# Engine queues written out task by task, and the weights' loads behind the second batch's x, in a spectral-filter and gated-unit kernel

## The chip, the cores and the metric

The kernel runs on one core of a Trainium2 chip. The metric is device time in microseconds (us) of one execution. Five engines matter: PE (TensorE, matmuls), DVE (VectorE), ACT (ScalarE), POOL (GpSimd, which here issues the loads of inputs) and SP (SyncE, which issues the scratch transfers and the stores). Each works through its own list of instructions in order and waits on semaphores for the others.

## What is computed

Eight batches of x, 3200 x 256, are filtered along the sequence by a real Fourier transform, a pointwise complex filter and the inverse transform. The result goes through a gated unit: a causal convolution of five taps per channel gives a gate, a sigmoid is taken of it, and it multiplies a projection; a second projection gives the output.

```python
X = np.fft.rfft(x, axis=1)
y = np.fft.irfft(X * (filt_r + 1j * filt_i)[None, :, :], n=x.shape[1], axis=1)
yp = np.concatenate([np.zeros((B, K - 1, D)), y], axis=1)
gate_pre = sum(conv_w[k] * yp[:, k:k + S, :] for k in range(K))
return (1 / (1 + np.exp(-gate_pre)) * (y @ w_val)) @ w_out
```

## The kernel before, in words

The transform of length 3200 is split as 100 x 32. For each batch b, in the names of the plan's tasks (the number after the comma counts the pieces):

- `lx` (L286, POOL): eight loads of x into `xt` tiles, of which there are ten, with a cast to bf16.
- `s1` (L548, PE): eight products of an x tile with the table cf_t. `so` (L539 on ACT, L541 on DVE): their evacuation from PSUM into one tile `so`.
- `t` (L567, DVE): four transposes of `so` into `tt`.
- `s2` (L577, PE), `xs` (L539 or L541), `z` (L593, DVE, multiplication with the filter tile f_t), `ia` (L608, PE, first half of the inverse) and `ue` (L539 or L541, evacuation into `u`): seven pieces each, the last one of half the size.
- The way from `u` to `vt`: batch 0 is turned by four transposes on DVE (`k`, L649). Batches 1 to 7 write `u` to a scratch in memory (`wr`, L631, SP) and read it back in another order (`lv`, L641 and L642, SP).
- `ib` (L659, PE) and `ye` (L668, ACT): the second half of the inverse, eight pieces, into `yt`. `ha` (L675, POOL) clears the four columns ahead of it.
- Then seven blocks of the sequence: `cv` (the convolution, L698, or L712 for pairs of blocks in batches 6 and 7), `ga` (sigmoid, L722, ACT), `vl` (L732, PE, reads the weights wv_t), `gv` (L747, DVE), `op` (L755, PE, reads the weights wo_t), `oe` (evacuation, L539 or L541) and `st` (store, L770, SP).

At the start there are tables to make (cf_t, w_t, a_t, b_t, ci_t, dg_t), the filters to load (L346, L349, L352, POOL, in two halves), and eight copies `fd` of filter halves to further partitions (ACT or DVE; they write f_t). `te` are the evacuations of a_t and b_t (`tp` are their matmuls), `dg` makes the ten small tables dg_t (L523, ACT), and `cim` makes ci_t (two products on DVE). `pd` (L624, POOL) clears a part of `u` for batch 0.

PSUM is used as four slots of 128 x 1024 in float32. Each PE task takes one (a pair of blocks takes two), and the evacuation gives it back. The tasks `so`, `xs`, `ue`, `oe`, `te` and `fd` may run on ACT or on DVE.

The order of instructions on every engine is made by a planner in the kernel's own program (class `Plan`), run once when the kernel is built. Each task has a cost per engine it may use, the tasks it depends on, buffers that it takes and gives, and a landing time for transfers. Before the change each task also has a rank, from a list of numbers TIMES. At each step the planner looks at all tasks that are ready and takes the one with the lowest rank, with a penalty STAY for a change of the PE array's mode and LEAN for DVE where ACT could do the task. The instructions are then written in that order with `manual_schedule`, which leaves it as it is. Transfers are planned on one line called DQ. These planned times are not measured ones; only the order reaches the chip.

The eleven weight loads are one task on POOL, `wts`, which the plan may begin, like the first x load of batch 1, when the task `pool` (a fixed number in the code) says that POOL is free. The order that results on POOL is: the filters' loads, `lx1,0`, `wts`, `lx1,1`, `pd0`, `lx1,2` and so on.

The first tasks that the queues hold before, where the change reaches them:

- DVE, after the tables: te3,0 fd0,0,0 t0,0 te1,0 fd0,1,1 t0,1 fd0,1,0 t0,2 fd1,0,0 cim t0,3 fd1,1,1 xs0,0 fd1,1,0 z0,0 z0,2 z0,1 ue0,2 z0,3 z0,4 z0,5 so1,2 xs0,6 z0,6 so1,4 k0,0 k0,1 k0,2 k0,3 t1,0
- PE, from the first s2: s20,0 s20,1 s11,0 s20,2 ia0,0 s20,3 ia0,2 s20,4 s11,1 ia0,1 s20,5 s11,2 ia0,3 s20,6 ia0,4 ia0,5 s11,3 s11,4 ia0,6 s11,5 s11,6 s11,7 ib0,0

(`s11,2` is piece 2 of s1 of batch 1, `s20,5` piece 5 of s2 of batch 0; `fd1,0,1` is the second half's first filter, second copy.)

Of the kernel before, what the change touches and what calls it, by code (L numbers as in the profile page):

```python
# [24 lines left out]
STAY, LEAN = 2.6, 5.1  # L25

TIMES = [6045, -2430, 3242, -301, 64, -3062, 3825, -4640, -1646, -3299, -5370, 2181, -2530, 351,
# [90 lines left out]
NCH = R // RC  # L118
# [828 lines left out]
```

## Time and profile before

| | |
|---|---|
| median of three runs | 304.4 us (303.82 to 306.0) |
| the profiled execution | 303.57 us, its span 301.8 us |
| busy: PE, DVE, ACT, POOL | 258.3, 263.6, 256.2, 63.0 us |
| granted TensorE clock, mean | 0.985 |
| transfers | 66.00 MB, mean 219 GB/s |

The span runs from the first to the last instruction; the time of the execution holds 1.8 us more around it. Busy time is what an engine spends in instructions. A matmul's end is modelled, so a busy PE need not be at its peak. In rows of the order of time the columns are start, length (both us), engine, line, operation, tiles written and read, count, and in brackets the idle time before it and what ended it. Rows of groups give the total busy time and the mean of one in ns.

### The profile page before, as it was taken

To read this page: it belongs to the slowest core of one execution; us is meant where nothing else is said; L and a number is where in the kernel's file an instruction comes from. 1 tells how busy PE (TensorE), PEld (TensorE's weight loads), DVE (VectorE), ACT (ScalarE), POOL (GpSimd) and SP (SyncE) were. 2 spreads that over 40 slices of the span, in tenths; PEclk is the share of its full clock that TensorE was granted. 3 is DMA by queue.
4 is the path that set the end of the run, shared out by engine and by line. 5 is a ranking of instruction groups with operands and counts; after the bars stand their busy time and mean duration, and the time that the engine had idled before them with its cause. 6 is when DMAs were issued, how large, how long until landed. Compare 5 with 4: busy or idle time off the path is not lost.

```text
span 301.8 us, 9355 instructions
## 1 busy us (share of the span) xinstructions
PE 258.3 (86%) x3924; PEld 156.8 (52%) x3924; DVE 263.6 (87%) x294; ACT 256.2 (85%) x299; POOL 63.0 (21%) x122
## 2 busy tenths in 40 slices
PE   2822492778999899989999999999999999999991
PEld 0111340634555654666466465747666677766661
DVE  7979959898999999999999999999999984766761
ACT  3997775699789997999999999999999889787652
POOL 8699953022023002300320300000000000000000
PEclk9999998799999999999999999999999999999998
DMA  6998699469689997999999997998563799875375
GB/s 91 190 112 103 79 166 186 79 94 182 173 244 269 252 305 179 222 282 359 198 237 316 289 212 205 331 311 288 174 231 121 233 292 341 280 292 208 125 292 204
DMA packets 52874, 66.00 MB, mean 219 GB/s; under 512 B 7712, under 2 KB 34208, under 8 KB 52832
## 3 DMA queue, kind: packets, MB, share of 16 engines
q1 hardware_dynamic: 40624, 50.09, 49.2%
q0 software_dynamic: 12208, 15.31, 32.7%
q8 instruction: 31, 0.51, 0.7%
q14 instruction: 11, 0.09, 0.1%
HBM read 42.54 MB, written 38.14 MB: 267 GB/s over the span
## 4 chain that ended last, share of the span: by engine, by line
PE 48%; DMA 14%; DVE 14%; POOL 9%; ACT 8%; issue 6%; SPq 0%; DVEq 0%; POOLq 0%; ACTq 0%
PE ps L755 11%; PE ps L698 11%; PE ps L732 11%; DMA vt<-escr 8%; PE ps L659 5%; PE ps L608 4%; DVE gv L747 3%; DVE so L541 3%; PE ps L712 3%; DMA out_dram<-o 3%; DMA f_t<-in_filt_r_dram 2%; PE ps L548 2%; POOL xt L286 2%; ACT so L539 2%; DVE vt L649 2%
## 5 line engine op out<-in xcount | busy, mean ns | idle before, releaser
L747 DVE TENSOR_TENSOR gv<-ps,gt 128x1024 bf16<-128x1024 f32 (+1 forms) x56 | 60.8, 1103 | 13.5 <-PE ps L732 10.1
L593 DVE TENSOR_TENSOR z<-xs,f_t 128x2048 bf16<-128x2048 bf16 (+1 forms) x56 | 62.7, 1138 | 4.3 <-ACT xs L539 4.1
L722 ACT ACTIVATE gt<-ps 128x1024 bf16<-128x1024 f32 (+1 forms) x56 | 52.1, 945 | 10.4 <-PE ps L712 5.8
L286 POOL DMA_DIRECT2D xt<-in_x_dram x64 | 36.4, 570 | 108.6 <-PE ps L548 89.3
L668 ACT ACTIVATE yt<-ps 128x800 bf16<-128x800 f32 x64 | 52.1, 846 | 7.0 <-PE ps L659 6.5
L548 PE MATMUL ps<-xt,cf_t 100*128 100x512 bf16 x128 | 43.5, 424 | 11.6 <-DMA xt<-in_x_dram 9.3
L755 PE MATMUL ps<-wo_t,gv 128*128 128x256 bf16 x400 | 51.8, 273 | 0.8 <-DVE gv L747 0.4
L732 PE MATMUL ps<-yt,wv_t 128*128 128x512 bf16 (+1 forms) x224 | 51.9, 356 | 0.0
L698 PE MATMUL ps<-yt,dg_t 64*64 64x512 bf16 (+1 forms) x880 | 48.7, 348 | 0.4
L539 ACT ACTIVATE so<-ps 128x1024 bf16<-128x1024 f32 x42 | 42.2, 1042 | 6.6 <-PE ps L548 4.2
L539 ACT ACTIVATE u<-ps 128x1024 bf16<-128x1024 f32 (+1 forms) x41 | 40.0, 982 | 4.7 <-PE ps L608 4.3
L755 PEld LDWEIGHTS <-gv 128*128 128x128 bf16 x400 | 36.8, 97 | 12.2 <-issue 3.0
L539 ACT ACTIVATE o<-ps 128x1024 f32<-128x1024 f32 (+1 forms) x37 | 36.8, 999 | 6.2 <-PE ps L755 5.3
L659 PE MATMUL ps<-ci_t,vt 104*128 104x100 f16 (+1 forms) x512 | 33.7, 213 | 8.8 <-DVE vt L649 6.5
L567 DVE STREAM_TRANSPOSE tt<-so 128x1024 f32<-128x1024 f32 x32 | 38.7, 1227 | 0.6 <-ACT so L539 0.6
L539 ACT ACTIVATE xs<-ps 128x1024 bf16<-128x1024 f32 (+1 forms) x36 | 35.3, 998 | 3.6 <-PE ps L577 3.3
L659 PEld LDWEIGHTS <-vt 104*128 104x128 bf16 (+1 forms) x512 | 28.4, 101 | 19.0 <-DVE vt L649 7.1
L698 PEld LDWEIGHTS <-dg_t 64*64 64x64 bf16 x880 | 24.3, 106 | 15.4 <-issue 4.3
L608 PE MATMUL ps<-z,a_t 64*64 64x256 bf16 x416 | 28.4, 289 | 4.5 <-ACT gt L722 1.9
L577 PE MATMUL ps<-tt,w_t 64*64 64x256 bf16 x416 | 23.5, 293 | 9.4 <-DVE tt L567 8.5
L608 PE MATMUL ps<-z,b_t 64*64 64x256 bf16 x416 | 28.1, 283 | 0.0
L732 PEld LDWEIGHTS <-wv_t 128*128 128x128 bf16 x224 | 19.0, 97 | 17.3 <-issue 3.2
(98 smaller groups left out, 225.1 us busy)
## 6 DMA issues: line engine op xcount, KB each, us to landing
out_dram<-o SPq DMA_DIRECT2D x48, 512.0 KB
xt<-in_x_dram POOLq DMA_DIRECT2D x64, 200.0 KB, 7.3
escr<-u SPq DMA_DIRECT2D x42, 256.0 KB
vt<-escr SPq DMA_DIRECT2D x56, 192.0 KB
out_dram<-o SPq DMA_DIRECT2D x8, 128.0 KB
escr<-u SPq DMA_DIRECT2D x7, 128.0 KB
vt<-escr SPq DMA_DIRECT2D x56, 16.0 KB
f_t<-in_filt_r_dram POOLq DMA_DIRECT2D x2, 112.0 KB, 3.6
```

The lines of the kernel that those rows point to most:

```text
L286: nc.gpsimd.dma_start(out=xt[0:L], in_=src)
L539: nc.scalar.activation(dst, src, AF.Copy, **kw)
L548: nc.tensor.matmul(ps[:, 512 * h:512 * h + 512], lhsT=cf_t[0:L].rearrange("p h c i -> p (h c i)"), rhs=xv[:, DQ // 2 * h:DQ // 2 * h + DQ ...
L593: nc.vector.tensor_tensor(z[:, :, :, 0:nm * D], st.pop(("XS", b, u))[:, :, 0:nm * D].unsqueeze(1) .to_broadcast((128, 2, 2, nm * D)), f_t[ ...
L608: nc.tensor.matmul(ps[64 * h:64 * h + 64, 512 * t + D * a:512 * t + D * a + D], lhsT=tab[rows, h, m0 + a, :], rhs=z[rows, w, h, D * a:D * ...
L659: nc.tensor.matmul(ps[:, o:o + L], lhsT=v[rows, RC * j + a, 128 * dh:128 * dh + 128], rhs=ci_t[rows, way, :], start=True, stop=True)
L668: nc.scalar.activation(y[:, :, H:H + N].rearrange("p h (a r) -> p h a r", r=R)[:, :, :, RC * j:RC * j + RC], ps[:, :].rearrange("p (h n) - ...
L698: nc.tensor.matmul(ps[o:o + 64, 512 * dh:512 * dh + w], lhsT=dg_t[rows, dh, k, :], rhs=y[rows, dh, BLK * c + k:BLK * c + k + w], start=(k ...
L722: nc.scalar.activation(g[:, :, 0:w], two_banks(ps, w), AF.Sigmoid)
L732: nc.tensor.matmul(ps[:, 512 * eh:512 * eh + w], lhsT=wv_t[:, dh, eh, o:o + 128], rhs=y[:, dh, H + BLK * c:H + BLK * c + w], start=(dh == ...
L747: nc.vector.tensor_tensor(o, i0, i1, op=ALU.mult)
L755: nc.tensor.matmul(ps[:, D * a:D * a + D], lhsT=gv_[:, eh, 128 * a:128 * a + 128], rhs=wo_t[:, c % 2 * pair(b, c), eh, :], start=(eh == 0) ...
```

## The change

The list of ranks and the choice among ready tasks go. In their place stand five lists, QUEUES, one each for PE, DVE, ACT, POOL and SP, that name the tasks (by their number in the order in which they are added) in the order in which the engine works them. So they also hold which of ACT and DVE does a task. The planner now only begins the first task of each line when it can, to find in which order to write out the instructions of the engines and which PSUM slot a task gets. Tasks without an engine and transfers are chosen as before.

The weights' task is split in two, `wv` (four loads) and `wo` (seven loads). In POOL's new queue `wv` stands behind `lx2,4` and `wo` behind `lx2,7`; before them come `lx1,0 pd0 lx1,1` to `lx1,7` and `lx2,0` to `lx2,4`. The first `vl` and the first `op` now depend on them in the plan. The first `s1` of a batch depends on the last one of the batch before. The landing times of the filters' parts, of the time at which POOL comes free and of the transfers' line are other numbers.

The new queues of the head, in the same names:

- DVE, after the tables: t0,0 t0,1 t0,2 t0,3 fd0,1,1 fd0,0,0 fd0,1,0 z0,0 fd1,0,0 z0,1 z0,2 fd1,1,0 fd1,0,1 fd1,1,1 z0,4 z0,3 z0,5 z0,6 ue0,5 k0,0 k0,1 k0,2 cim k0,3 t1,0
- PE, from the first s2: s20,0 tp2 s20,1 ia0,0 s20,2 s20,3 ia0,1 s11,0 ia0,2 s20,4 s20,5 s11,1 ia0,4 s20,6 ia0,3 ia0,5 ia0,6 s11,2 s11,3 s11,4 s11,5 s11,6 s11,7 ib0,0
- ACT, from the last so of batch 0: fd0,0,1 te1,0 te0,0 te1,1 te0,1 xs0,0 cia te2,0 xs0,1 te2,1 te3,0 xs0,2 xs0,3 ue0,0 ue0,1 so1,0 xs0,4 xs0,5 te3,1 ue0,2 xs0,6 ue0,4 ue0,3 ue0,6 dg0 so1,3 so1,2 so1,1 so1,4 so1,6 so1,5 so1,7 ye0,0

Over the whole kernel the tasks that stand in ACT's queue go from 289 to 299, in DVE's from 237 to 227; `so` goes from 42 to 52 on ACT and from 22 to 12 on DVE, and the copy `fd1,0,1` goes from ACT to DVE. PE's 406 tasks are the same, in another order.

```diff
 SMALL = (6, 7)
-STAY, LEAN = 2.6, 5.1
-TIMES = [6045, -2430, 3242, -301, 64, -3062, 3825, -4640, -1646, -3299, -5370, 2181, -2530, 351,
...
+QUEUES = dict(
+    PE=[0, 2, 4, 6, 8, 10, 12, 1557, 14, 1554, 1563, 21, 1560, 26, 24, 31, 36, 29, 142, 34, 41,
+           46, 146, 44, 51, 39, 49, 54, 150, 154, 158, 162, 166, 170, 60, 62, 64, 66, 68, 70, 177,
...
+    DVE=[1549, 1551, 1553, 1566, 16, 17, 18, 19, 1543, 1540, 1542, 23, 1544, 28, 33, 1546, 1545,
...
+    ACT=[1550, 3, 5, 7, 1, 9, 1552, 13, 1570, 11, 15, 1541, 1558, 1555, 1559, 1556, 22, 1567,
...
+    POOL=[140, 20, 144, 148, 152, 156, 160, 164, 168, 338, 342, 346, 350, 354, 1521, 358, 362, 76,
...
+    SP=[182, 190, 198, 206, 214, 230, 222, 83, 234, 252, 237, 240, 243, 249, 92, 246, 255, 404,
...
-    def __init__(self, room, slots, times, stay=1.0, lean=0.0):
-        self.tasks, self.room, self.stay = {}, dict(room), stay
-        self.lean, self.slots, self.times = lean, list(range(slots)), iter(times)
+    def __init__(self, room, slots, queues):
+        self.tasks, self.room, self.queues = {}, dict(room), queues
+        self.slots = list(range(slots))
 
     def add(self, name, engines, deps, emit, take=(), give=(), land=0.0, mode=None,
             ps=0, free=()):
-        queue = engines.keys() - {"none", "DQ"}
-        rank = next(self.times) / 100 if queue else 0.0
-        self.tasks[name] = dict(engines=engines, rank=rank, deps=deps, emit=emit, take=take,
+        self.tasks[name] = dict(engines=engines, deps=deps, emit=emit, take=take,
                                 give=give, land=land, mode=mode, ps=ps, free=free, slots=[],
                                 at=len(self.tasks))
 
     def run(self):
+        names = list(self.tasks)
+        lines = {e: [names[i] for i in q] for e, q in self.queues.items()}
...
+        def can(n):
+            t = self.tasks[n]
+            return (need[n] == 0 and ready_at[n] <= now + 1e-9 and len(self.slots) >= t["ps"]
+                    and all(self.room[p] >= t["take"].count(p) for p in t["take"]))
+
+        def begin(n, e):
...
-            best = None
-            for n in ready:
...
-                for e, cost in t["engines"].items():
-                    if free.get(e, 0.0) <= now + 1e-9:
-                        away = e == "PE" and t["mode"] != mode
-                        other = e == "DVE" and len(t["engines"]) > 1
-                        key = (round(t["rank"] + (self.stay if away else 0.0)
-                                     + (self.lean if other else 0.0), 6), cost, t["at"])
...
+            went = left
+            for n in [n for n in loose["none"] if can(n)]:
+                if can(n):
+                    loose["none"].remove(n)
+                    begin(n, "none")
+            if left < went:
...
+            for e, line in lines.items():
+                if line and free.get(e, 0.0) <= now + 1e-9 and can(line[0]):
+                    begin(line.pop(0), e)
...
-    def load_w():
+    def load_wv():
         for dh in range(2):
             src = moe_w_val[128 * dh:128 * dh + 128, :].rearrange("p (e j) -> p e j", e=2)
             nc.gpsimd.dma_start(out=wv_t[:, dh, :, 0:128], in_=src)
             nc.gpsimd.dma_start(out=wv_t[:, dh, :, 128:224], in_=src[:, :, 0:96])
+
+    def load_wo():
         for s in range(2):
...
-    plan = Plan(dict(xt=NXT, so=1, t=1, xs=3, z=3, u=1, e=2, v=1, y=2, g=NGB, gv=NGB, o=NOB), 4, TIMES,
-                stay=STAY, lean=LEAN)
+    plan = Plan(dict(xt=NXT, so=1, t=1, xs=3, z=3, u=1, e=2, v=1, y=2, g=NGB, gv=NGB, o=NOB), 4, QUEUES)
...
-                add(f"lx{b},{j}", {"POOL": 0.6}, ["pool"] + ([f"lx{b},{j - 1}"] if j else [f"lx{b - 1},{NCH - 1}"] if b > 1 else []),
+                add(f"lx{b},{j}", {"POOL": 0.6}, ["pool"] + (
+                    [f"lx{b},{j - 1}"] if j else [f"lx{b - 1},{NCH - 1}"] if b > 1 else []),
                     lambda e, b=b, j=j: load_x(b, j), take=("xt",), land=1.5)
                 add(f"dx{b},{j}", {"DQ": 1.22}, [f"lx{b},{j}"], None, land=2.0, mode=1)
             dep = [f"dx{b},{j}"] if b else [f"x0{j}", "cfa"]
-            dep = dep + ([f"s1{b},{j - 1}"] if j else [])
+            dep = dep + ([f"s1{b},{j - 1}"] if j else [f"s1{b - 1},{NCH - 1}"] if b else [])
             add(f"s1{b},{j}", {"PE": 0.45}, dep, lambda e, b=b, j=j: s1(b, j),
...
-                [f"cv{b},{p}"] + ([f"vl{b},{c - 1}"] if c else []), lambda e, b=b, c=c: val(b, c),
+                [f"cv{b},{p}"] + ([f"vl{b},{c - 1}"] if c else [] if b else ["wvq+"]), lambda e, b=b, c=c: val(b, c),
...
-            add(f"op{b},{c}", {"PE": 0.88 * f}, [f"gv{b},{c}"],
+            add(f"op{b},{c}", {"PE": 0.88 * f}, [f"gv{b},{c}"] + ([] if b or c else ["woq+"]),
...
-    add("pool", {"none": 0.0}, [], None, land=22.0)
-    add("wts", {"POOL": 5.0}, ["pool"], lambda e: load_w())
+    add("pool", {"none": 0.0}, [], None, land=24.4)
+    add("wv", {"POOL": 4.2}, ["pool"], lambda e: load_wv())
+    dma("wvq", 2.4, ["wv"], land=2.0, mode=1)
+    add("wo", {"POOL": 3.4}, ["wv"], lambda e: load_wo())
+    dma("woq", 2.6, ["wo"], land=2.0, mode=1)
     for j in range(NCH):
         add(f"x0{j}", {"none": 0.0}, [], None, land=4.5 + 1.3 * j)
-    add("dq", {"DQ": 23.5}, [], None, mode=0)
-    for n, when in (("fr0,0", 16.5), ("fr0,1", 19.6), ("fr1,0", 22.8), ("fr1,1", 25.8)):
+    add("dq", {"DQ": 25.5}, [], None, mode=0)
+    for n, when in (("fr0,0", 16.3), ("fr0,1", 20.0), ("fr1,0", 23.3), ("fr1,1", 27.0)):
         add(n, {"none": 0.0}, [], None, land=when)
```

More of the change, by code (lines that the diff above doesn't have):

```diff
@@ L144, in run @@
     def run(self):
-        left = dict(self.tasks)
+        names = list(self.tasks)
+        lines = {e: [names[i] for i in q] for e, q in self.queues.items()}
         users, need = {}, {}
-        for n, t in left.items():
+        for n, t in self.tasks.items():
             need[n] = len(t["deps"])
@@ L150, in run @@
                 users.setdefault(d, []).append(n)
-        ready_at = {n: 0.0 for n in left}
-        free = {}
+        ready_at = {n: 0.0 for n in names}
+        loose = {e: [n for n in names if e in self.tasks[n]["engines"] and need[n] == 0]
+                 for e in ("none", "DQ")}
+        free, gives, order = {}, [], []
         mode = turn = None
-        gives = []
-        ready = {n for n in left if need[n] == 0}
-        order = []
-        now = 0.0
+        now, left = 0.0, len(names)
+        def can(n):
[3 more added lines that the diff above has]
+        def begin(n, e):
+            nonlocal mode, turn, left
+            t = self.tasks[n]
+            cost = t["engines"][e]
+            for p in t["take"]:
+                self.room[p] -= 1
+            t["slots"] = [self.slots.pop(0) for _ in range(t["ps"])]
+            if e == "PE":
+                cost += 0.1 if t["mode"] != mode else 0.0
+                mode = t["mode"]
+            if e == "DQ":
+                turn = t["mode"]
+            end = now + cost
+            done = end + SEM.get(e, 0.1)
+            if e != "none":
+                free[e] = end
+            back = list(t["give"]) + [self.tasks[o]["slots"][i] for o, i in t["free"]]
+            if back:
+                gives.append((done, back))
+            for u in users.get(n, ()):
+                need[u] -= 1
+                ready_at[u] = max(ready_at[u], done + t["land"])
+                for k in loose:
+                    if need[u] == 0 and k in self.tasks[u]["engines"]:
+                        loose[k].append(u)
+            left -= 1
+            order.append((t["emit"], e, t["slots"], now, end))
         while left:
@@ L190, in run @@
-            if best is None:
-                later = [ready_at[n] for n in ready if ready_at[n] > now + 1e-9]
-                later += [v for v in free.values() if v > now + 1e-9]
-                later += [g[0] for g in gives if g[0] > now + 1e-9]
-                assert later, ("stuck", sorted(ready)[:20], self.room)
-                now = min(later)
-                continue
-            _, n, e, cost = best
-            t = left.pop(n)
-            ready.discard(n)
-            for p in t["take"]:
-                self.room[p] -= 1
@@ L202, in run @@
-            t["slots"] = [self.slots.pop(0) for _ in range(t["ps"])]
-            if e == "PE":
-                if t["mode"] != mode:
-                    cost += 0.1
-                mode = t["mode"]
-            if e == "DQ":
-                turn = t["mode"]
-            end = now + cost
-            free[e] = end
-            done = end + SEM.get(e, 0.1)
-            back = list(t["give"]) + [self.tasks[o]["slots"][i] for o, i in t["free"]]
-            if back:
-                gives.append((done, back))
@@ new lines, in run @@
+            for e, line in lines.items():
+                if line and free.get(e, 0.0) <= now + 1e-9 and can(line[0]):
+                    begin(line.pop(0), e)
+            if free.get("DQ", 0.0) <= now + 1e-9:
+                here = [n for n in loose["DQ"] if can(n)]
+                if here:
+                    n = min(here, key=lambda n: (
+                        round(ready_at[n] + (1e4 if self.tasks[n]["mode"] == turn else 0.0), 6),
+                        self.tasks[n]["at"]))
+                    loose["DQ"].remove(n)
+                    begin(n, "DQ")
@@ L221, in run @@
+            if left < went:
+                continue
+            later = [v for v in free.values() if v > now + 1e-9] + [g[0] for g in gives]
+            later += [ready_at[n] for n in loose["none"] + loose["DQ"]]
+            later += [ready_at[line[0]] for line in lines.values() if line and need[line[0]] == 0]
+            later = [v for v in later if v > now + 1e-9]
+            assert later, ("stuck", {e: line[:1] for e, line in lines.items()}, self.room)
+            now = min(later)
         self.span = max(free.values())
@@ L912 @@
         sp_setup()
-        for emit, e, slots in order:
+        for emit, e, slots, _, _ in order:
             st["slots"] = list(slots)
```

22 lines of the change are left out of this document (removed), and 158 rows, old and new, of tables (ACT, DVE, PE, POOL).

## The prediction

> **What bounds the kernel now.** I read the page first, for the load of each engine, then the busy time by stretches, for where each is full.
>
> ```profile
> span 301.8 us, 9355 instructions
> PE 258.3 (86%) x3924; PEld 156.8 (52%) x3924; DVE 263.6 (87%) x294; ACT 256.2 (85%) x299; POOL 63.0 (21%) x122
> ```
>
> ```profile
> 27.30:46.90 19.60, 14.32 (x171) 7.49 (x172) 15.28 (x15) 13.74 (x16) 15.66 (x26) 1.00 0.88 127
> 46.90:60.00 13.10, 6.08 (x77) 4.78 (x76) 11.96 (x9) 7.51 (x10) 1.37 (x4) 0.74 0.70 128
> 60.00:210.00 150.00, 142.32 (x2092) 83.89 (x2087) 146.16 (x135) 140.97 (x164) 21.48 (x42) 1.00 0.92 246
> 210.00:250.00 40.00, 40.00 (x684) 26.78 (x674) 38.34 (x38) 37.42 (x44) 0.21 (x2) 1.00 0.65 218
> 250.00:290.00 40.00, 39.97 (x814) 27.54 (x813) 25.58 (x25) 30.04 (x35) 0.10 (x1) 1.00 0.69 252
> 290.00:301.80 11.80, 5.26 (x40) 3.33 (x38) 3.11 (x4) 4.90 (x5) 0.00 (x0) 0.90 0.58 226
> ```
>
> Three engines carry nearly the same load. The columns of the second view are window, length, then busy time of PE, weight loads, DVE, ACT and POOL. From 60 to 210 DVE is the fullest (146.2 of 150), from 210 to 290 PE is never idle, and the end (from 290) is a drain. The empty time is at the head: from 27.3 to 60 PE works 20.4 of 32.7 us. A head that ends earlier brings the full part forward by as much, unless the full part itself grows.
>
> Who sets the pace in the head is told by the order of time on POOL, PE, DVE and ACT:
>
> ```profile
> 24.49 1.33 POOL L286 DMA_DIRECT2D xt<-in_x_dram  x1
> 25.81 0.76 POOL L359 DMA_DIRECT2D wv_t<-in_moe_w_val_dram  x1
> 27.26 1.33 POOL L359 DMA_DIRECT2D wv_t<-in_moe_w_val_dram  x1
> 29.27 1.65 POOL L365 DMA_DIRECT2D wo_t<-in_moe_w_out_dram  x2
> 33.63 0.56 POOL L286 DMA_DIRECT2D xt<-in_x_dram  x1 [0.16 <-issue]
> 34.17 1.40 POOL L624 MEMSET u<- 128x1536 bf16 x1
> 35.50 4.38 POOL L286 DMA_DIRECT2D xt<-in_x_dram  x8
> ```
>
> ```profile
> 27.38 1.07 PE L577 MATMUL ps<-tt,w_t 64*64 64x256 bf16 x16 [8.52 <-DVE tt L567]
> 37.35 1.03 PE L548 MATMUL ps<-xt,cf_t 100*128 100x512 bf16 x2 [2.45 <-DMA xt<-in_x_dram]
> 54.18 3.92 PE L659 MATMUL ps<-ci_t,vt 128*128 128x100 f16 x55 [3.25 <-DVE vt L649]
> ```
>
> ```profile
> 18.20 1.25 DVE L567 STREAM_TRANSPOSE tt<-so 128x1024 f32<-128x1024 f32 x1 [0.58 <-ACT so L539]
> 24.62 1.08 DVE L541 COPY f_t<-f_t 32x3584 bf16<-32x3584 bf16 x1
> 25.72 0.46 DVE L303 TENSOR_SCALAR ci_t<-sx,wt 128x100 f16<-128x100 f32 x2
> 26.08 1.24 DVE L567 STREAM_TRANSPOSE tt<-so 128x1024 f32<-128x1024 f32 x1
> 27.35 1.09 DVE L541 COPY f_t<-f_t 32x3584 bf16<-32x3584 bf16 x1
> 41.41 1.23 DVE L593 TENSOR_TENSOR z<-xs,f_t 128x2048 bf16<-128x2048 bf16 x1 [3.16 <-ACT xs L539]
> 46.90 3.71 DVE L649 STREAM_TRANSPOSE vt<-u 128x1024 f32<-128x1024 f32 x2 [0.44 <-ACT u L539]
> ```
>
> ```profile
> 22.31 1.29 ACT L523 ACTIVATE dg_t<-j,cw 128x64 bf16<-128x64 f16 x5
> 39.43 1.02 ACT L539 ACTIVATE u<-ps 128x1024 bf16<-128x1024 f32 x1 [3.10 <-PE ps L608]
> 46.66 2.89 ACT L539 ACTIVATE so<-ps 128x1024 bf16<-128x1024 f32 x3
> 54.98 2.29 ACT L668 ACTIVATE yt<-ps 128x800 bf16<-128x800 f32 x3 [5.43 <-PE ps L659]
> ```
>
> Two things stretch the head. First, PE idles 8.52 us because the four turns of batch 0 (L567) run from 18.20 to 27.32 on DVE: filter copies and other work stand between them in DVE's queue. Second, eleven weight loads hold POOL from 25.81 to 33.5, so the second x tile of batch 1 is issued at 33.63 and PE, which works its queue in order, waits 2.45 us for it at 37.35. That wait is handed on: ACT idles 3.10 and DVE 3.16 behind it. The next fixed point is 46.90, where batch 0's second turn (L649) begins.
>
> **The change, part by part.** Durations come from the groups, shapes kept apart:
>
> ```profile
> L567 DVE STREAM_TRANSPOSE tt<-so 128x1024 f32<-128x1024 f32 x32 | 38.7, 1227 | 0.6 <-ACT so L539 0.6
> L593 DVE TENSOR_TENSOR z<-xs,f_t 128x2048 bf16<-128x2048 bf16 x48 | 57.4, 1216 | 4.2 <-ACT xs L539 4.1
> L541 DVE COPY f_t<-f_t 32x3584 bf16<-32x3584 bf16 x3 | 3.3, 1084 | 0.1
> L541 DVE COPY f_t<-f_t 32x3072 bf16<-32x3072 bf16 x3 | 3.0, 991 | 0.1
> L539 ACT ACTIVATE f_t<-f_t 32x3584 bf16<-32x3584 bf16 x1 | 3.2, 3187 | 0.0
> L593 DVE TENSOR_TENSOR z<-xs,f_t 128x1024 bf16<-128x1024 bf16 x8 | 5.3, 668 | 0.1
> L539 ACT ACTIVATE so<-ps 128x1024 bf16<-128x1024 f32 x42 | 42.2, 1042 | 6.6 <-PE ps L548 4.2
> L541 DVE CAST so<-ps 128x1024 bf16<-128x1024 f32 x22 | 26.2, 1216 | 1.3 <-ACT yt L668 1.1
> ```
>
> *Head, DVE's queue.* The new queue puts the four turns first and the filter copies behind them. The turns wait for the last so evacuation as before, so they start at 18.2 and end at 18.2 + 4 x 1.23 = 23.1 in place of 27.3. Between the first turn and L649 the new queue holds 4 turns (4.91), 3 first-half copies (2.97), all 4 second-half copies (4.34; one came from ACT, where it took 3.19), 6 full z (7.30), the short z (0.67) and one u evacuation (1.2): 21.4 us. The old queue held 24.7 there and took 46.90 - 18.20 = 28.7, so 4.0 of it was idle (3.16 in one piece, behind the x wait). With no idle L649 would begin at 39.6, 7.3 earlier; with the same 4.0, at 43.6, 3.3 earlier. The x wait should go, but DVE still depends on ACT and on four PSUM slots, so I take the middle: 5.3 earlier. The two ci_t products (0.46) move into the middle of the L649 turns, which gives back 0.5: **-4.8**.
>
> *Head, behind that point.* ACT must now do dg_t (1.29) and seven so of batch 1 (0.96 each by the run of three) between L649's start and the first yt: 8.0 us. Before, the first yt began 54.98 - 46.90 = 8.1 after it. Nothing is gained or lost here: 0, between -0.5 and +0.5.
>
> *x tiles of batch 1.* Seven issues and the 1.40 memset follow the filters at once, from 25.8: the second tile about 27.2 in place of 33.63. It was used 3.7 us after issue (33.63 to 37.35), so it can be used from 31. In the new PE queue that tile's matmuls stand behind the second half of the s2 and ia work, which z paces to past 33. The 2.45 wait goes, inside the -4.8.
>
> *Weights.* The value weights now stand behind the thirteenth x issue after batch 0 (the fifth tile of batch 2), which needs the buffer of batch 1's third tile; PE reads that right before L649's start, at about 41. The four issues took 25.81 to 29.27, 3.5 us; the output weights' seven took 29.27 to 33.5, 4.2 us, and follow the last x of batch 2. Landing took 4.1 and 4.3 us:
>
> ```profile
> wv_t<-in_moe_w_val_dram POOLq DMA_DIRECT2D x2, 48.0 KB, 4.1
> wo_t<-in_moe_w_out_dram POOLq DMA_DIRECT2D x1, 64.0 KB, 4.3
> 73.08 1.04 PE L732 MATMUL ps<-yt,wv_t 128*128 128x512 bf16 x4
> ```
>
> Value weights are there by 41 + 0.6 + 3.5 + 4.1 = 49, output weights by about 57. The first reader was at 73.08 and comes to 68: 19 us of cover. Behind them on POOL the last three x of batch 2 come 3.5 later and batch 3's first 4.2 later; both are read 8 us and more after that. Cost 0; were the cover gone, the eleven issues would cost up to 7.7.
>
> *The steady part.* Nothing is added for PE: 406 tasks in both, and the mode of the array changes 143 times for 147. ACT and DVE exchange work. Ten so move from DVE to ACT; u and xs move about as much between them. By the groups' means, over the whole kernel DVE loses 9.7 us and ACT gains 6.5. Of this DVE loses 5.1 between its last L649 turn and batch 4's last gv (54 to 240), and ACT gains 4.3 between the first yt of batch 0 and of batch 6 (55 to 244). If DVE alone bound the stretch it would shrink by 5.1; if ACT did, it would grow by 4.3. From 60 to 210 DVE has 146.2 now and would have about 141, ACT 141.0 and would have 145.3: the fullest engine falls by 0.9. I take **-0.9**.
>
> Here a rule decides whether PE matters. PE is 95% busy from 60 to 210 with 2092 matmuls in 150 us, 13.9 per us, and 100% busy from 210 to 250 with 17.1 per us: the same share hides a different pace. The Trainium skill (Perfetto Trace Analysis, Identifying the Most-Contended Engine) says that matmul busy time is a poor measure of headroom, because matmuls are pipelined, and that weight-load time is better; the trace agrees, with 83.9 of 150 against 26.8 of 40 (56 and 67%). By plain PE busy time the steady part would change by 0 and the sum be 0.9 higher.
>
> *Tail.* Two of the last ten PE tasks change places, and the last two stores: 0, within 0.4.
>
> *Filter landings planned as measured.* They are only numbers for the planner; they act through the order, already counted.
>
> **Sum.** The profiled execution took 303.57 (span 301.8 and 1.8 around it). 303.57 - 4.8 - 0.9 = 297.9. It lies 0.83 below the median of the three runs, 304.4, so I predict 298.7.
>
> **Rivals.**
> *DVE's relief counts in full.* Then the middle gives -5.1 for -0.9: 304.4 - 4.8 - 5.1 = 294.5. For it: DVE 146.2 of 150. Against: ACT takes most of the work and is nearly as full.
>
> *ACT becomes the bound and gives the head back.* 304.4 - 4.8 + 4.3 = 303.9, no change. For it: all eight so of batches 1 and 5 on ACT, and ACT's 9 us of slack from 60 to 210 halved. Against: DVE may wait instead; half the slack is left.
>
> *The x tiles are still late.* POOL issues took 1.33 at 24.49 and at 27.26, both beside an f_t copy on DVE (24.62, 27.35), and 0.55 each in the run of eight at 35.50. The new queue runs three copies from 23.1 and four among the first z, while POOL issues filters and x. Four issues held 0.78 each make 3.1 us, which uses up the 2 us between 31 and 33 and brings back a wait, at most the old 2.45: 304.4 - 2.35 - 0.9 = 301.2. Against: these copies were there before and only cluster now. The Trainium skill (SBUF — State Buffer, Who interferes with whom) states this as a lock: a DVE copy in a two-port mode shuts GpSimd out of the shared port for the whole instruction, and so stalls its descriptors; the trace agrees, with 1.33 beside copies against 0.55.
>
> *Slower: PE's held order waits for reloads.* The order is fixed to planned times, and PE cannot pass a task whose data is late. Batches 1 to 7 each reload vt from memory before L659.
>
> ```profile
> PE ps L659 <- DMA vt<-escr: 1.0, 1, 1.0
> ```
>
> Now PE waits 1.0 once. To be 1% slower, the kernel must lose 3.0 + 5.7 = 8.7 us: 1.25 at each of seven reloads. From there it is slower; 1.4 each gives 304.4 - 5.7 + 9.8 = 308.5. For it: the DMA engines are busy 0.92 of 60 to 210. Against: the old order is just as fixed, and hardly waits.
>
> **Chances and range.** Forecast 0.50 (own range 295.5 to 301); DVE's relief 0.13; ACT 0.15; late x 0.08; reloads 0.14. A measurement of this kernel can tell about 1% from no change: 301.4 and 307.4. Faster: 0.50 + 0.13 + half of late x = 0.67; within 1%: 0.15 + 0.04 = 0.19; slower 0.14. The range, 294 to 304.4, reaches from the full DVE relief to ACT as the bound and leaves out the reloads.
>
> **What would show it.** First L577 on PE at 23 to 24 (now 27.38); no wait for xt of over 0.5 us on PE between 27 and 45; L649 on DVE starting between 39.6 and 43.6; the first yt about 8.1 later; no wait of L732 or L755 for wv_t or wo_t; DVE near 254 and ACT near 263 busy; from batch 1's first reload on, the same length as before. Wrong if L649 starts after 44, if PE waits for vt<-escr at several batches, or if ACT stands at 98% and PE idles over 10 us from 55 to 205.

## The result, and the profile after

| | before | changed |
|---|---|---|
| median | 305.0 us (303.82 to 306.19, 12 runs) | 303.13 us (300.73 to 305.84, 12 runs) |
| the profiled execution | 303.57 us, span 301.8 | 304.79 us, span 302.5 |
| busy: PE, DVE, ACT | 258.3, 263.6, 256.2 us | 261.0, 257.2, 260.8 us |

The ratio of the changed kernel to the one before is 0.9929, 95% interval 0.9904 to 0.9955. That is 2.2 us less (the medians differ by 1.9); 5.7 were forecast. Ratios here and below leave out slow runs, those over 1.5% above the fastest of the same kernel: two of the changed kernel's twelve (305.26 and 305.84), and some runs of four later versions. The two profiled executions cannot be subtracted: that of before lies 1.4 us below its median, that of the changed kernel 1.7 above its own. So I compare stretches, not ends. Line numbers of the changed kernel are ten lower than before (L649 is now L639), and twelve lower ahead of the queues (L286 is now L274); in the experiments' kernels they are one lower still, in one of them two.

The page's head, then the busy time by stretches (window, length, then PE, weight loads, DVE, ACT, POOL):

```profile
span 302.5 us, 9314 instructions
PE 261.0 (86%) x3924; PEld 158.8 (53%) x3924; DVE 257.2 (85%) x284; ACT 260.8 (86%) x309; POOL 62.1 (21%) x122
```

```profile
23.00:42.26 19.26, 12.06 (x179) 7.22 (x180) 17.91 (x15) 14.93 (x22) 11.19 (x14) 0.91 0.92 147
55.00:145.00 90.00, 85.16 (x1225) 49.59 (x1222) 84.16 (x77) 85.92 (x99) 16.56 (x33) 0.99 0.87 217
145.00:170.00 25.00, 20.82 (x291) 12.10 (x288) 20.13 (x20) 19.30 (x24) 2.51 (x5) 0.93 0.91 269
170.00:210.00 40.00, 39.05 (x572) 23.84 (x574) 38.94 (x37) 38.60 (x47) 2.85 (x6) 1.00 0.78 228
```

The kernel before, in the stretch that matters:

```profile
145.00:170.00 25.00, 24.54 (x349) 14.15 (x348) 24.96 (x24) 23.98 (x30) 4.68 (x10) 1.00 1.03 273
```

Between 145 and 170 all three engines were full before; now each has 4 to 6 idle us. No other stretch has such a hole.

*The head did what was forecast.* The order of time on PE, DVE, ACT and POOL:

```profile
23.00 0.64 PE L567 MATMUL ps<-tt,w_t 64*64 64x256 bf16 x8 [5.25 <-DVE tt L557]
36.25 0.60 PE L538 MATMUL ps<-xt,cf_t 100*128 100x512 bf16 x2 [0.49 <-ACT xs L529]
67.40 1.02 PE L722 MATMUL ps<-yt,wv_t 128*128 128x512 bf16 x4
```

```profile
42.26 5.53 DVE L639 STREAM_TRANSPOSE vt<-u 128x1024 f32<-128x1024 f32 x3
50.81 4.49 ACT L658 ACTIVATE yt<-ps 128x800 bf16<-128x800 f32 x6 [1.31 <-PE ps L649]
24.59 1.40 POOL L614 MEMSET u<- 128x1536 bf16 x1
25.92 6.49 POOL L274 DMA_DIRECT2D xt<-in_x_dram  x9
```

The first s2 begins at 23.00 (27.38 before), the second turn at 42.26 (46.90), the first yt at 50.81 (54.98), the first value product at 67.40 (73.08). The wait for x is gone. From 55 to 145 no engine has a hole like the one after 145, and the lead holds.

*It is lost at one place.* The chain of waits, of the changed kernel, from 146:

```profile
146.49 1.14 DVE z L583
147.63 0.32 SPq L621
147.95 0.04 issue
147.99 9.87 DMA out_dram<-o
...
157.98 1.24 DVE o L531
159.22 0.04 issue
159.26 1.02 PE ps L722 x4
```

The same place in the order of time: three evacuations into output buffers (`o`), SP's queue, and then DVE, PE and ACT.

```profile
94.89 1.05 ACT L529 ACTIVATE o<-ps 128x1024 f32<-128x1024 f32 x1
142.44 1.07 ACT L529 ACTIVATE o<-ps 128x1024 f32<-128x1024 f32 x1
134.61 1.21 DVE L531 COPY o<-ps 128x1024 f32<-128x1024 f32 x1
```

```profile
142.98 0.34 SPq L632 DMA_DIRECT2D vt<-escr  x1
147.57 0.38 SPq L621 DMA_DIRECT2D escr<-u  x1
147.99 2.86 SPq L760 DMA_DIRECT2D out_dram<-o  x3
```

```profile
157.98 1.23 DVE L531 COPY o<-ps 128x1024 f32<-128x1024 f32 x1 [3.62 <-DMA out_dram<-o]
159.26 1.02 PE L722 MATMUL ps<-yt,wv_t 128*128 128x512 bf16 x4 [2.69 <-DVE o L531]
160.63 1.02 ACT L529 ACTIVATE o<-ps 128x1024 f32<-128x1024 f32 x1 [4.32 <-PE ps L649]
```

How to read this: SP, too, works its queue in order. After the reload at 142.98 its next entry is wr4,0, the write of batch 4's first piece of `u`, which leaves only at 147.57. What it waits for shows in DVE's order of time and in the table of SP's waits between 86 and 152 (what was waited for, us in total, times, the longest):

```profile
144.14 2.35 DVE L531 CAST u<-ps 128x1024 bf16<-128x1024 f32 x2
SPq L621 <- DMA vt<-escr: 4.4, 2, 4.2
```

The piece of `u` is the first of the two in this row, so it is there at about 145.4. The 4.2 us on SP end later, with the landing of a reload. In the trace, SP's transfers signal on eight semaphores in turn, and an entry waits until the transfer eight ahead of it has landed. For wr4,0 that is the reload issued at 140.37, and it landed at 147.5. So wr4,0 was held first by its data and then, for some 2 us, by a landing. The chain of waits names a z on DVE in that place, which wr4,0 does not read; it is only what ended nearest. One expectation below puts the hold down to ue4,0, the evacuation of this piece, alone; that is not so.

Behind wr4,0 stand three stores whose data had long been ready: st0,4 since 95.9 (it left at 96.2 before), st1,5 since 135.8 and st1,4 since 143.5. They leave at 147.99, 149.65 and 150.09, the second and the third again each behind the landing of a reload. There are four output buffers; a fourth evacuation at 153.9 takes the last one. So DVE's next evacuation cannot start until the first store has landed, at 157.86, 9.87 us after its issue. DVE works in order as well and stands 3.62 us. It holds a PSUM slot, so PE stands 2.69, and ACT 4.32 behind PE.

My theory (S): a store held in SP's in-order queue keeps an output buffer, and that gives back most of the head's gain. Rivals: transfers crowd each other there whatever their order (C; the first expectations call it R); a lead in the head cannot be kept, whatever SP does, because ACT is the bound (A).

### The profile page after: what moved, and what is told of

Its sections match the earlier page's. It is cut to its first block, busy times and chain, and to the rows that moved or that the text cites. A ratio compares the mean times of both kernels' runs of the same rounds, so it can differ in the third digit from the quotient of the medians.

```text
span 302.5 us, 9314 instructions
## 1 busy us (share of the span) xinstructions
PE 261.0 (86%) x3924; PEld 158.8 (53%) x3924; DVE 257.2 (85%) x284; ACT 260.8 (86%) x309; POOL 62.1 (21%) x122
## 4 chain that ended last, share of the span: by engine, by line
PE 54%; DVE 19%; ACT 11%; issue 4%; DMA 3%; DVEq 0%; SPq 0%; ACTq 0%
PE ps L745 12%; PE ps L722 12%; PE ps L688 10%; PE ps L649 5%; PE ps L598 5%; DVE z L583 4%; DVE gv L737 4%; PE ps L538 4%; DMA out_dram<-o 3%; PE ps L567 3%; ACT xs L529 3%; DVE u L531 3%; PE ps L702 3%; DVE vt L639 2%; DVE tt L557 2%
## 5 line engine op out<-in xcount | busy, mean ns | idle before, releaser
L737 DVE TENSOR_TENSOR gv<-ps,gt 128x1024 bf16<-128x1024 f32 (+1 forms) x56 | 61.7, 1107 | 13.7 <-PE ps L722 11.5
L712 ACT ACTIVATE gt<-ps 128x1024 bf16<-128x1024 f32 (+1 forms) x56 | 51.4, 938 | 10.2 <-PE ps L702 6.2
L274 POOL DMA_DIRECT2D xt<-in_x_dram x64 | 37.7, 592 | 106.1 <-PE ps L538 103.2
L529 ACT ACTIVATE so<-ps 128x1024 bf16<-128x1024 f32 x52 | 51.8, 1038 | 5.6 <-PE ps L538 5.1
L745 PEld LDWEIGHTS <-gv 128*128 128x128 bf16 x400 | 37.6, 98 | 13.2 <-issue 3.7
L529 ACT ACTIVATE o<-ps 128x1024 f32<-128x1024 f32 (+1 forms) x37 | 35.4, 962 | 9.9 <-PE ps L649 4.3
L529 ACT ACTIVATE xs<-ps 128x1024 bf16<-128x1024 f32 (+1 forms) x38 | 37.2, 998 | 4.5 <-PE ps L567 4.3
L529 ACT ACTIVATE u<-ps 128x1024 bf16<-128x1024 f32 (+1 forms) x38 | 36.7, 976 | 2.3 <-PE ps L598 2.3
L649 PE MATMUL ps<-ci_t,vt 104*128 104x100 f16 (+1 forms) x512 | 33.7, 217 | 4.3 <-DVE vt L639 1.6
L649 PEld LDWEIGHTS <-vt 104*128 104x128 bf16 (+1 forms) x512 | 28.9, 103 | 15.1 <-issue 5.3
L531 DVE COPY o<-ps 128x1024 f32<-128x1024 f32 (+1 forms) x19 | 20.0, 1050 | 10.8 <-PE ps L745 5.8
L567 PE MATMUL ps<-tt,w_t 64*64 64x256 bf16 x416 | 22.7, 292 | 6.8 <-DVE tt L557 5.6
```

Source lines behind the costliest of these rows:

```text
L529: nc.scalar.activation(dst, src, AF.Copy, **kw)
L649: nc.tensor.matmul(ps[:, o:o + L], lhsT=v[rows, RC * j + a, 128 * dh:128 * dh + 128], rhs=ci_t[rows, way, :], start=True, stop=True)
L712: nc.scalar.activation(g[:, :, 0:w], two_banks(ps, w), AF.Sigmoid)
L737: nc.vector.tensor_tensor(o, i0, i1, op=ALU.mult)
L745: nc.tensor.matmul(ps[:, D * a:D * a + D], lhsT=gv_[:, eh, 128 * a:128 * a + 128], rhs=wo_t[:, c % 2 * pair(b, c), eh, :], start=(eh == 0) ...
```

## The experiments

Short diffs show the numbers in the queues. 119 is st0,4, 101 st0,2, 326 st1,5, 317 st1,4, 776 wr4,0, 792 wr4,2, 626 wr3,6, 630 lv3,0; 636, 639, 645 and 651 are four reloads of batch 3 (lv3,2 lv3,3 lv3,5 lv3,7).

**One store moved** (the changed kernel):

```diff
-    SP=[... 110, 396, 101, 412, ... 633, 630, 776, 119, 326, 317, 784, ...
+    SP=[... 110, 396, 101, 119, 412, ... 633, 630, 776, 326, 317, 784, ...
```

> The changed kernel with one store moved: that of batch 0, block 4, goes in SP's queue from behind the first u write of batch 4 (issued at 148 us in the profiled run, its data ready at 96) to behind the store of batch 0, block 2. Theory S (late stores hold the four output buffers, so an evacuation on DVE waits for a landing and everything stands behind it): the wait for out_dram on DVE shrinks or goes, the stretch 150 to 170 is fuller, 2 to 5 us less than the changed kernel, ratio to the kernel before 0.978 to 0.987. Rival R (transfers crowd around 150 us and anything that needs one waits): within 0.3% of the changed kernel's 0.993. Rival A (ACT became the bound): 0.993 too.

300.57 us (299.95 to 300.76, 4 runs) against 305.48: 0.9835, 0.9807 to 0.9863. The same stretch and DVE's order of time:

```profile
145.00:170.00 25.00, 22.83 (x326) 13.29 (x328) 24.01 (x24) 23.49 (x28) 4.62 (x10) 1.00 1.02 289
```

```profile
153.75 1.77 DVE L530 COPY o<-ps 128x256 f32<-128x256 f32 x2
```

Both evacuations now follow each other without a wait, as forecast by S. Moving one entry of one queue brings 1%, and the median is 4.9 us less than that of the kernel before. wr4,0 also left earlier here, at 145.20, right behind its data, since the reload it waits for had landed at 144.2; the other two stores left at 145.6 and 147.5; what part of the 1% that brings is not told apart. PE still waits 1.1 us for vt of batch 3 here. That ACT binds the kernel is refuted: its load is the same (260.9).

**All late stores moved**: sixteen stores that were more than 5 us late go to where their data is ready; nothing else differs from the changed kernel.

> The changed kernel with all sixteen stores that left over 5 us after their data was ready moved forward in SP's queue to where they were ready; nothing else. Theory S: no wait of an engine for out_dram before 250 us, ratio to the kernel before 0.975 to 0.985 (the head's 4.6 us kept, and no loss). Rival R: 0.993, or worse if the earlier stores slow the reloads. Rival A: 0.993 with ACT near 98% from 60 to 210.

302.23 us (6 runs): 0.9895, 0.986 to 0.9931. The forecast of S, 0.975 to 0.985, was missed; the interval overlaps that of the changed kernel. There is no store wait before 250, but there are three after it, two of them on DVE:

```profile
260.64 1.23 DVE L530 COPY o<-ps 128x1024 f32<-128x1024 f32 x1 [1.83 <-DMA out_dram<-o]
268.12 0.42 DVE L530 COPY o<-ps 128x256 f32<-128x256 f32 x1 [2.64 <-DMA out_dram<-o]
```

The third is 0.81 us on ACT at 265. And PE waits 3.1 us for reloads of vt between 55 and 300, against 1.4 with one store moved. So early is no good by itself. That a store which wasn't needed early went ahead of a transfer that was is my reading; no run shows it alone.

**Stores held in the kernel before**: its own order, written as queues, with the three stores put behind a later write. There are two doses, wr4,2 and then wr4,0:

```diff
-    SP=[... 101, 380, 110, 119, ... 626, 326, 299, 317, 618, ... 636, 792, 642, 648, 776, ...
+    SP=[... 101, 380, 110, ... 626, 299, 618, ... 636, 792, 119, 326, 317, 642, 648, 776, ...
...
+    SP=[... 101, 380, 110, ... 626, 299, 618, ... 636, 792, 642, 648, 776, 119, 326, 317, ...
```

> The kernel before, its own orders written as queues, with three stores held: those of batch 0, block 4 and of batch 1, blocks 5 and 4 go behind the first u write of batch 4 on SP (issued at 156 us before; data ready at 96, 139 and 141). Theory S: all four output buffers are out when the first output evacuation of batch 2 comes at 161, it waits some 3 to 7 us, ratio to the kernel before 1.007 to 1.022. Rival R and rival A: 1.00 within 0.3%.

> The kernel before with the same three stores as in e4_before_held, now behind the second u write of batch 4 on SP (issued at 159.6 before). In e4 they left 7 to 9 us ahead of the evacuation that wanted a buffer, and nothing waited. Theory S with a landing of 8 to 10 us: they leave at 160, land at 168 to 170, and the second output evacuation of batch 2, at 163 to 164, waits 4 to 6 us; ratio 1.005 to 1.018. If holding stores does no harm here either, 1.00 within 0.3%, and S rests on e1 alone.

PE, DVE, ACT and POOL keep the order of the kernel before; only SP's differs. The first: 0.9996, 0.997 to 1.0021; the forecast loss (1.007 to 1.022) did not come. The second: 307.47 us, 1.0093, 1.0059 to 1.0126, as forecast. SP's stores in the first and the second, and ACT's wait in the second:

```profile
155.08 1.90 SPq L759 DMA_DIRECT2D out_dram<-o  x3
```

```profile
158.86 4.51 SPq L759 DMA_DIRECT2D out_dram<-o  x3
166.03 1.02 ACT L528 ACTIVATE o<-ps 128x1024 f32<-128x1024 f32 x1 [1.62 <-DMA out_dram<-o]
```

The first three left 4 us earlier and had landed when a buffer was wanted (164.1 on ACT). By these two doses, holding costs nothing until the landing passes that moment; then it costs. So the hold is enough to slow a kernel with the old orders too, by its size and not by its being there. The wait on ACT was shorter than forecast (1.62 us, for 4 to 6), and the loss is 2.8 us; the rest of it is not traced to a row.

**Reloads ahead of the blocked write**, on top of the one store moved. It would take away PE's 1.1 us wait for vt:

```diff
-    SP=[... 633, 630, 776, 326, 317, 784, 636, 639, 800, 645, 651, 792, ...
+    SP=[... 633, 630, 636, 639, 645, 651, 776, 326, 317, 784, 800, 792, ...
```

> As e1_one_store, with the last four reloads of batch 3 on SP ahead of the first u write of batch 4, which held them from 143 to 152 us. If PE's remaining wait for vt there (1.1 us in e1) is on the path: 0.3 to 0.5% below e1, 0.979 to 0.981. If the steady part is bound by the engines' work: 0.9835 within 0.3%. If reloads and stores crowd each other: above it.

305.03 us (12 runs): 0.9965, 0.9934 to 0.9996. None of the forecasts without crowding came true: the time was to be that of the one store moved or less, and most of the gain is lost again.

```profile
153.82 1.22 SPq L759 DMA_DIRECT2D out_dram<-o  x2
160.08 1.02 ACT L528 ACTIVATE o<-ps 128x1024 f32<-128x1024 f32 x1 [4.17 <-DMA out_dram<-o]
```

PE's wait for vt went, but st1,5 and st1,4 went from 145.6 and 147.5 to 153.8 and just behind, and ACT waited 4.17 for a buffer. The reloads were not quick to leave either: the trace has them from 147.5 to 151.9, each held till an earlier transfer had landed. By itself all this was as well explained by rival C. The next pair tells them apart.

**Three stores moved, and then the reloads behind them:**

```diff
-    SP=[... 626, 618, 586, 610, 299, 648, 642, 633, 630, 776, 326, 317, 784, 636, 639, ...
+    SP=[... 626, 326, 618, 586, 610, 299, 648, 642, 633, 630, 317, 776, 784, 636, 639, ...
...
+    SP=[... 626, 326, 618, 586, 610, 299, 648, 642, 633, 630, 317, 636, 639, 645, 651, 776, 784, ...
```

> The changed kernel with three stores moved in SP's queue: st0,4 behind st0,2 (as in the version with one store moved), st1,5 behind wr3,6 and st1,4 behind lv3,0, so that none of the three stands behind wr4,0 any more. Theory S (a store behind SP's in-order wait for ue4,0 holds an output buffer; one freed buffer is enough): as with one store moved, 0.98 to 0.988 of the kernel before (299 to 301.5 us), no wait of an engine for out_dram between 145 and 170, and PE still waits about 1 us for vt of batch 3 near 160. Rival C (earlier stores compete with the reloads for the DMA engines, as with all sixteen moved): 0.988 to 0.992, a longer wait of PE for vt<-escr near 160 than the 1.08 us with one store moved.

> The version with three stores moved, with four reloads of batch 3 (lv3,2 lv3,3 lv3,5 lv3,7) ahead of wr4,0 too, behind st1,4. The stores now leave ahead of the reloads; with the stores behind the reloads the store wait had come back and the ratio was 0.9965. Theory S (what cost time there was that the stores were held, not the reloads themselves): neither the wait for out_dram nor that for vt<-escr between 145 and 170, 0.975 to 0.986 of the kernel before (297.5 to 300.7 us). Rival C (the stores and reloads crowd each other on the DMA engines in any order): the wait for out_dram at 160 comes back with over 2 us, ratio 0.99 to 1.0.

Three stores: 300.53 us, 0.9849, 0.9819 to 0.9879, as with one, and no wait for a store. Stores and then reloads: 300.11 us, 0.9842, 0.9807 to 0.9877, with neither wait in that stretch; this row is of that version:

```profile
145.00:170.00 25.00, 23.89 (x342) 14.19 (x335) 24.57 (x25) 24.43 (x29) 5.06 (x10) 1.00 1.04 283
```

The same reloads ahead of the same write give 0.9965 when the stores stand behind them and 0.9842 when they stand ahead. That refutes C at this place: the order counts, not the crowd. Here st1,4 still left only at 147.5, 4 us after its data was ready and with no blocked write ahead of it: it, too, waited for the landing of a reload. The hole is filled (PE 23.89 of 25). In the profiled executions batch 3's last inverse product begins 1.4 us earlier than with one store moved, but the medians do not tell the three versions apart.

**What each half of the head is worth.** Three kernels: the weights alone, in the old orders; the turns undone, with the one store moved; the weights back behind lx1,0, with all late stores moved.

```diff
-    POOL=[140, 1521, 1524, 144, 20, 148, ... 354, 358, 362, 366, 536, ...
+    POOL=[140, 20, 144, 148, ... 354, 1521, 358, 362, 366, 1524, 536, ...
...
-    DVE=[... 16, 17, 18, 19, 1543, 1540, 1542, 23, 1544, 28, ...
+    DVE=[... 1540, 16, 1543, 17, 1542, 18, 1544, 19, 23, 28, ...
...
-    POOL=[140, 20, 144, 148, ... 354, 1521, 358, 362, 76, 366, 1524, 536, ...
+    POOL=[140, 1521, 1524, 20, 144, 148, ... 354, 358, 362, 76, 366, 536, ...
```

(140 is lx1,0, 144 lx1,1, 20 the memset pd0, 1521 and 1524 the weights; 16 to 19 are the four turns, 1540 to 1544 filter copies, 23 and 28 the first z.)

> The kernel before, its own orders, with only POOL's queue changed: value weights behind the fifth x load of batch 2, output weights behind its last, and the memset of u ahead of batch 1's second x load. Theory T, in which the weights count only where PE's order reads x early, as the old order does: PE's 2.45 us wait for x goes and batch 0's second turn starts 1.5 to 3 us before 46.9; ratio 0.990 to 0.996. Rival W, the loads make the whole head: 4 us and more, 0.987 or less. A third reading, that something else ends at 46.9 anyway: 1.00 within 0.3%.

> As e1_one_store, but on DVE the four turns of batch 0 stand among the filter copies as in the kernel before (copy, turn, copy, turn, copy, turn, copy, turn); weights stay late. Theory T (turns put first give the head): the turns end near 26 to 27, PE's first s2 starts near 27, batch 0's second turn 1.5 to 4 us later than the 42.3 of e1, and the time 0.5 to 1.3% above e1 (0.9835), so 0.988 to 0.997. Rival W (the weights' move gives the head): second turn at 42.3 within 0.7 and 0.9835 within 0.3%.

> As e2_stores_early, but the eleven weight loads stand on POOL where the kernel before has them, behind the first x load of batch 1; every other queue stays. Theory W (the move of the loads gives part of the head): the wait of PE for x comes back, batch 0's second turn starts 1 to 3 us later than in the changed kernel (42.3), and the time is 0.3 to 1.0% above e2. Rival T (the turns put first give all of the head): turn at 42.3 within 0.5, same time as e2 within 0.3%.

The weights alone: 303.04 us, 0.9925 (0.9904 to 0.9946); POOL issues lx1,1 at 27.33 and the second turn begins at 45.35 in place of 46.90. The turns undone: 302.77 us, 0.9927 (0.9903 to 0.9951), against 0.9835 with the turns first. The weights back: 302.2 us, 0.9911 (0.9882 to 0.994), against 0.9895 without that. In this order the rows of the three:

```profile
27.33 7.10 POOL L273 DMA_DIRECT2D xt<-in_x_dram  x10
45.35 5.45 DVE L638 STREAM_TRANSPOSE vt<-u 128x1024 f32<-128x1024 f32 x3 [0.33 <-ACT u L528]
```

```profile
27.63 0.64 PE L565 MATMUL ps<-tt,w_t 64*64 64x256 bf16 x8 [9.37 <-DVE tt L555]
43.88 5.53 DVE L637 STREAM_TRANSPOSE vt<-u 128x1024 f32<-128x1024 f32 x3
162.58 1.39 PE L647 MATMUL ps<-ci_t,vt 104*128 104x100 f16 x16 [2.11 <-DMA vt<-escr]
```

```profile
36.72 0.62 PE L537 MATMUL ps<-xt,cf_t 100*128 100x512 bf16 x2 [2.52 <-DMA xt<-in_x_dram]
41.82 1.97 DVE L638 STREAM_TRANSPOSE vt<-u 128x1024 f32<-128x1024 f32 x1
```

In the old orders the weights' move, with the memset that goes along with it, is worth 0.75%, and the second turn comes 1.55 us earlier, as forecast. Undoing the turns costs 0.9%, about 2.8 us: 1.6 us at the second turn (43.88 for 42.27) and some of it at a reload for which PE waits 2.11, where it waited 1.08 with the turns first. But with the turns first the weights' move is worth nothing that these runs can tell: 0.9911 and 0.9895 have overlapping intervals. The wait for x comes back on PE in full (2.52), and the second turn still begins at 41.82, not later than the 42.50 of the same kernel without it, as rival T of the expectation has it. DVE has the filter copies to do in that time (4.32 us for three, then four z without a wait), so PE's wait is beside the path. One thing is mixed in: with the weights back, the memset of `u` also runs later, from 31.17, and the first three copies take 2.85 us instead of 4.71, the three later ones 4.32 instead of 3.21. The net 0.75 is about what the turn came earlier. So the weights' own worth with the turns first is not measured apart from the memset.

**The memset moved.** The trace had one more row out of line. The three 32x3072 copies took 4.7 us in place of 3.0, one of them 2.85 in place of 0.95, and in that time POOL's memset of `u` runs (24.59 to 25.99). In the version with stores and then reloads:

```diff
-    POOL=[140, 20, 144, 148, 152, 156, 160, 164, 168, ...
+    POOL=[140, 144, 148, 152, 156, 160, 164, 20, 168, ...
```

> The version with stores, then reloads, with one more edit: POOL's memset of u (pd0) goes from behind lx1,0 to behind lx1,6. In the changed kernel and in every version since, one filter copy on DVE (fd0,0,0) that runs beside this memset took 2.3 to 2.8 us in place of 0.95 and ends 0.8 us after the memset; DVE is nearly full from there to the second turn (L638). Theory M (the memset holds the copy, and the copy lies on the path of the head): the three 32x3072 copies take 2.9 us together in place of 4.7, the second turn starts at about 40.0 in place of 41.7, and the kernel takes about 0.5% less than the same version without the edit: 0.976 to 0.982. Rival N (the xs evacuations on ACT and the products on PE set the pace of the head, so DVE only waits elsewhere): copies shorter, but the second turn at 41.4 or later and the ratio as without the edit.

> The version with stores, then reloads, once more beside the one with the memset moved, on the same chip: 0.9842 again within its interval by either theory (0.98 to 0.988); it is the value that the memset's move is compared with.

298.38 us: 0.9763, 0.973 to 0.9796; beside it, without the edit, 299.87 us: 0.9809, 0.9776 to 0.9842. The profiled execution of the first took 303.56 us, 4 us more than any of its six others, so only its head is read here. DVE in the version with the memset moved, and then without:

```profile
23.35 2.81 DVE L530 COPY f_t<-f_t 32x3072 bf16<-32x3072 bf16 x3
27.51 2.04 DVE L530 COPY f_t<-f_t 32x3584 bf16<-32x3584 bf16 x1
41.46 5.53 DVE L638 STREAM_TRANSPOSE vt<-u 128x1024 f32<-128x1024 f32 x3
```

```profile
23.28 4.71 DVE L530 COPY f_t<-f_t 32x3072 bf16<-32x3072 bf16 x3
29.34 1.08 DVE L530 COPY f_t<-f_t 32x3584 bf16<-32x3584 bf16 x1
42.58 5.50 DVE L638 STREAM_TRANSPOSE vt<-u 128x1024 f32<-128x1024 f32 x3
```

The copies get back 1.9 us, and the next copy, at 27.51, now took 2.04 for 1.08 beside x issues on POOL. The second turn comes at 41.46, where M expected about 40.0 and its rival N 41.4 or later. It is 1.1 earlier than in the trace beside it, but the same unedited version, profiled before, had it at 41.71, so the turn decides nothing. The medians differ by 1.5 us, as M expected, though the two intervals still overlap. So that the memset's move gains 0.5% is likely and not shown; the rows show only that the copies are shorter without it. This version has the lowest median of all. A fifth output buffer, which could show the held stores from the other side, was not tried.

## Why the prediction was wrong, point by point

- *What bounds the kernel, and the head:* right. The turns ended at 23.0 (forecast 23.1), the second turn began at 42.26 (forecast 41.6, between 39.6 and 43.6). The first yt came 8.55 behind it, for 8.1, and so 4.2 earlier than before; 4.8 was forecast. The idle time was smaller than the 2.0 that I left in (1.35: 17.91 of 19.26 busy), and the copies' 1.9 beside the memset, which I had not seen, took its place. So that 41.6 came so near has a share of luck: two errors of opposite sign. I weighed the lock between DVE and POOL only as a danger to POOL's issues.
- *x tiles and weights:* the times were right, the cover too: no wait for wv_t or wo_t. The reason may be half wrong. I put the x wait inside the 4.8; in the trace with the weights back and the turns first, that wait lies beside DVE's path. How much of the 4.8 hangs on the loads is not shown, since the memset moved with them.
- *The steady part, -0.9:* this is the step that failed. It weighed three engines' loads (DVE fell by 6.4 and ACT rose by 4.6, for 9.7 and 6.5) and took the stretch to be as long as its fullest engine is busy. It put SP's queue and the four output buffers that its stores hold at nothing, without looking, though the change writes that queue out as well. There one store moved from 96.2 to 148.0, and DVE waited 3.62 us for its landing. The loss is 1% by the kernel with one store moved (0.9929 to 0.9835), some 2.9 us; in the two profiled executions, of which that of the changed kernel is a long one, it is 4.2 us. With that store freed the gain is 4.9 us, 4.2 to 5.9 by the interval, which the forecast 5.7 fits. Whether -0.9 holds by itself none of the runs can tell.
- *Tail, landings:* nothing seen, as forecast.
- *Rivals:* the one that ended slower had the right kind of cause, a held order that cannot pass an entry whose data is late, on the wrong engine and transfer: PE and a reload, where it was SP and a store. ACT as the bound is refuted by the kernel with one store moved, late x by the rows.
- *What would show it:* its signs in the head held. The loads of DVE and ACT did not come to where they were expected (257.2 and 260.8, for about 254 and 263), and the last sign failed, "from batch 1's first reload on, the same length as before".

What stays open: why the changed kernel's own times spread over 5 us (300.73 to 305.84) where with one store moved they spread over 0.8 (4 runs). The store's landing, on which it waits, could explain that; one profile of each does not show it. The other versions do not settle it: with the reloads ahead, where a store is waited for too, twelve runs spread over 6.1 us, but with the weights back they spread over 5.8, and no store is waited for there in that stretch.

## What to carry to other kernels

When an order is written out by hand or by a planner, read every queue that it changes, the transfers' issuing queue too: for each entry, what is it waiting for (its data, a buffer, or the landing of an earlier transfer), and what that is long ready stands behind it? A late store costs nothing until its buffer is wanted, so compare issue plus landing with the next use of the buffer, not with the moment when the data was ready. And test a gain in the head against the first place downstream where a fixed order meets a transfer.

## What the runs showed of the hardware

- Of three 512 KB stores issued within 2.1 us (147.99, 149.65, 150.09), the first took 9.87 us from issue to landing. In the same kernel x loads of 200 KB took 6.5 in the median.
- An issuing queue keeps a transfer whose data is ready behind one that waits: st0,4, with its data ready at 95.9, left at 147.99 behind wr4,0. In these kernels such a wait is also for the landing of the transfer eight ahead: with the reload of 140.37 landing at 147.5, wr4,0 left at 147.57.
- A DVE copy and a POOL memset hold each other up. The copies' row in the changed kernel, and then the memset and the copy beside it in the weights-alone kernel:

```profile
L531 DVE COPY f_t<-f_t x7: 949/1083/2845, 23.0 to 35.0; 32x3584 bf16<-32x3584 bf16 x4, 32x3072 bf16<-32x3072 bf16 x3
```

```profile
25.15 2.23 POOL L613 MEMSET u<- 128x1536 bf16 x1
24.73 1.33 DVE L530 COPY f_t<-f_t 32x3584 bf16<-32x3584 bf16 x1
```

The memset took 1.40 in the changed kernel and 2.23 there, beside a copy that took 1.33 for 1.08. The 32x3072 copy took 0.95 alone and 2.85 in the changed kernel (the maximum of the first row). The Trainium skill (SBUF — State Buffer, Who interferes with whom) says that a DVE instruction in a two-port mode contends with GpSimd, that whoever issues first holds the shared ports for its whole instruction, and that the other is fully blocked. The trace agrees that either may be the one that waits. It does not agree on who: in the changed kernel the copy began first, at 23.96 against the memset's 24.59, and it was the copy that was held up.
